# Causal attention and an FFN on one core: scores with queries on partitions, and DMA transposes of the exponentials

## The chip, the core and the metric

The kernel runs on one core of a Trainium2 chip. A core has five engines that run side by side, each with its own in-order queue of instructions: TensorE (PE) for matrix products, with the loading of its weights (PEld) shown apart; VectorE (DVE); ScalarE (ACT); GpSimd (POOL); and SyncE (SP), which here issues all DMAs. Engines wait for each other by semaphores. TensorE writes to PSUM, eight banks of 128 partitions by 512 float32 columns; the rest lives in SBUF, also in 128 partitions. A matrix product takes a weight tile of up to 128 x 128, and streams the columns of a second operand past it.

The metric is the device time of one execution in microseconds (us).

## What is computed

Eight sequences (B) of 576 tokens (S), eight heads (H) of 64 (D): causal softmax attention, mixed by a gate with a read from a memory; then a feed-forward network on all 4608 tokens. Inputs and weights are float32 or float64, and products are made of float16 parts that together hold more digits.

```python
def _attn_ref(q, k, v, M_prev, z_prev, beta):
    scores = scale * np.matmul(q, k.transpose(0, 1, 3, 2))
    scores = np.where(causal, -1000000000.0, scores)
    scores = scores - scores.max(-1, keepdims=True)
    a = np.exp(scores)
    a /= a.sum(-1, keepdims=True) + 1e-09
    local = np.matmul(a, v)
    q_p = phi(q)         # phi(x) = max(x, 0) + min(exp(x), 1)
    mem_out = einsum(q_p, M_prev) / (einsum(q_p, z_prev) + 1e-06)
    return g * mem_out + (1 - g) * local

def _moe_ref(x, w_in, w_out):          # x: 4608 x 512, w_in: 512 x 2048, w_out: 2048 x 512
    h = x @ w_in
    g = h * np.clip(h + 3.0, 0.0, 6.0) / 6.0
    return g @ w_out
```

## The kernel before

**Attention.** Queries go in blocks of 128 (the fifth of a sequence has 64). Heads come in pairs. A unit is some query blocks of one head: blocks 0 and 1 together, or one of blocks 2, 3, 4, so that a unit's scores fill one PSUM bank. A sequence has 4 x 8 = 32 units, in the order unit kind, pair, head. For sequences 1 to 7 the operands are float16: k and q as high and low parts, stacked so that one product with 128 rows holds both of k's parts. Sequence 0 runs in float32 while the weights are prepared.

A unit goes through these steps, each a method of `Unit`:

- `scores` (PE, L347, L348, L350): keys on the output's partitions, queries on its columns. For each block i and each key block j up to i, two products of 128 (or 64) columns; on the diagonal a third adds the mask (identity by `negm`). One of three banks (`ps_s`) holds the result, sT.
- `reduce` (DVE L360, ACT L358, POOL L362): the maximum over the key blocks, per partition and query; then a maximum over the partitions, which POOL also spreads to all of them (mb).
- `sub` (DVE L368): a = sT + shift - mb. `exp` (ACT L377) in place, and the high part ah in float16 (POOL L381).
- `lo` (DVE L389): the low part, al = a - ah.
- `pv` (PE L413 to L417): ah and al stand with keys on partitions, and so are weights for the products with v as they are. Per block and key block three products of 64 or 65 columns; then two with the memory. The 65th column of v is ones: the sum of the row.
- `combine` (DVE L430 to L432, L438; ACT L436, L437): division, gate, sum into x, for both heads of a pair.

**Preparation.** While a sequence runs, `prep_steps` brings the next one's pairs: loads of q, k, v (SP), absolute maxima (ACT, POOL), scales (DVE), splits into parts (ACT and DVE, L156, L157), and copies by DMA into one of six slots (four for k as `stack`, L210 and L211, four for q, L218, four for phi(q)). `PREP_AT` says in which unit each step is emitted.

**FFN.** 18 blocks of 256 tokens. A block has 16 pieces: 8 of `ffn1` (L523 to L525, 24 products of 256 columns each; then ACT L531, DVE L532, ACT L533, DVE L534), 8 of `ffn2` (L546 to L548, 12 products of 512 columns). Block 0 is float32. Its x comes as two float16 parts, moved to the transposed place by `dma_start_transpose` (SP, L496). W1 and W2 arrive as float64 words, are decoded on ACT and DVE (L622 to L626) and split (L157).

**Order.** The main loop emits, for unit t, its scores and reduction, for unit t-1 sub, exp and lo, for unit t-2 pv and combine, and in between FFN pieces at an even rate, attention `LEAD` = 40 pieces ahead. `at(...)` gives each piece of work a priority, and the Tile framework's scheduler makes of that the order of instructions on each engine. The last 80 pieces of the FFN are left to the end.

Of the kernel before, what the change touches and what calls it, by code (L numbers as in the profile page):

```python
# [12 lines left out]
F32 = mybir.dt.float32  # L13
# [40 lines left out]
PREP_AT = (  # L54
# [4 lines left out]
)  # L59
PREP_AT_0 = (  # L60
    (10, 11, 12, 12, 13, 14, 14, 15, 15, 15),
    (16, 17, 18, 18, 19, 19, 20, 20, 21, 21),
) + PREP_AT[2:]
LN_SA = float(np.log(SA))


@with_exitstack
def kernel(ctx, tc, qT, kT, v, mz, beta, w_in, w_out, out):
# [249 lines left out]
    class Unit:  # L318
# [56 lines left out]
        def exp(self):  # L375
            a = self.a[:, 0:self.n]
            ACT.activation(a, a, AF.Exp, scale=slots[self.b, self.p]["esc"])  # L377
            if self.b == 0:
                return
# [429 lines left out]
```

## Time and profile before

| | |
|---|---|
| runs | 1120.56 and 1121.33 us, median 1120.94 us |
| profiled execution | 1120.2 us from its first to its last instruction |
| ScalarE busy | 791.1 us (71%) |
| GpSimd busy | 412.2 us (37%) |
| HBM, DMA | 48.14 MB read, 9.44 MB written; 101.39 MB moved, mean 91 GB/s |

The profile is of one execution. The runs' times hold some tenths of a microsecond around the span. A group's row has: line, engine, operation, what it writes and reads, shapes, count, then busy time and the mean of one in ns, then the idle time of the engine just ahead of such instructions and what ended it. The row of slices shows the course: 40 slices of 28 us, each digit the busy share in tenths.

```profile
PE   8999999999999899999999999999999999999998
PEld 6888767586767667676768576867685868685664
DVE  5999889899899969998999988888799968893321
ACT  5787879677877778787877787668686857563321
POOL 3322223444444433554244533354344433341000
DMA  8734452333424343315332434233404230101100
```

DVE's load is near full until the last quarter, in which the attention has ended and the FFN alone runs on. Matmuls overlap each other, so that a full row of PE is not PE at its peak.

### The profile page before, as it was taken

What the parts mean: (1) busy time and instruction counts of PE and PEld (TensorE: products, weight loads), DVE (VectorE), ACT (ScalarE), POOL (GpSimd) and SP (SyncE); (2) the same over time, 40 slices, a digit from 0 to 9 for tenths busy, and PEclk for the clock granted to TensorE, in tenths of its full rate; (3) what the DMA queues carried; (4) which work ended last, traced back from release to release, by engine and by line L of the source; (5) the groups of instructions that cost most, each with busy time, mean ns of one, the idle gap of its engine ahead of it and who ended that gap; (6) DMA issues with size and microseconds to landing.
All of it is one profiled execution on the core that took longest, in us unless ns stands there. A gap on an engine that the chain in (4) does not pass through costs nothing.

```text
span 1120.2 us, 28768 instructions
## 1 busy us (share of the span) xinstructions
PE 1083.2 (97%) x10736; PEld 797.4 (71%) x10736; DVE 930.7 (83%) x2436; ACT 791.1 (71%) x1880; POOL 412.2 (37%) x544
## 2 busy tenths in 40 slices
PE   8999999999999899999999999999999999999998
PEld 6888767586767667676768576867685868685664
DVE  5999889899899969998999988888799968893321
ACT  5787879677877778787877787668686857563321
POOL 3322223444444433554244533354344433341000
PEclk9999999999999999999999999999999999999999
DMA  8734452333424343315332434233404230101100
GB/s 263 291 100 160 119 135 70 94 91 87 116 84 106 70 118 89 97 45 138 97 76 71 101 96 102 76 92 97 116 22 107 77 69 14 36 5 36 27 13 19
DMA packets 101468, 101.39 MB, mean 91 GB/s; under 512 B 50256, under 2 KB 80976, under 8 KB 101328
## 3 DMA queue, kind: packets, MB, share of 16 engines
q1 hardware_dynamic: 101328, 99.56, 33.1%
q8 instruction: 84, 1.38, 0.5%
q14 instruction: 56, 0.46, 0.1%
HBM read 48.14 MB, written 9.44 MB: 51 GB/s over the span
## 4 chain that ended last, share of the span: by engine, by line
PE 42%; DVE 32%; ACT 8%; issue 8%; DMA 6%; POOL 2%; SPq 1%; DVEq 0%; ACTq 0%; POOLq 0%
DVE a L368 6%; PE po L546 5%; PE po L548 5%; PE po L547 5%; PE ph L523 5%; DVE rm L360 5%; PE ph L524 4%; PE ph L525 4%; DVE al L389 4%; DVE r L532 3%; PE ph L518 3%; DVE g L534 2%; PE sT L343 2%; DVE W L157 2%; POOL mb L362 2%
## 5 line engine op out<-in xcount | busy, mean ns | idle before, releaser
L362 POOL PARTITION_ALL_REDUCE mb<-rm x256 | 251.7, 983 | 336.7 <-DVE rm L360 237.4
L523 PE MATMUL ph<-x,W 128*128 128x256 f16 x1088 | 297.6, 274 | 12.7 <-DVE r L532 7.3
L525 PE MATMUL ph<-x,W 128*128 128x256 f16 x1088 | 297.5, 273 | 0.0
L524 PE MATMUL ph<-x,W 128*128 128x256 f16 x1088 | 297.4, 273 | 0.0
L381 POOL TENSOR_SCALAR_AFFINE_SELECT ah<-a 128x384 f16<-128x384 f32 (+2 forms) x224 | 145.4, 650 | 214.4 <-ACT a L377 105.4
L546 PE MATMUL po<-W,g 128*128 128x512 f16 x544 | 206.6, 380 | 1.9 <-ACT ot L554 1.6
L548 PE MATMUL po<-W,g 128*128 128x512 f16 x544 | 206.5, 380 | 0.8 <-DVE g L534 0.8
L547 PE MATMUL po<-W,g 128*128 128x512 f16 x544 | 206.7, 380 | 0.0
L377 ACT ACTIVATE a<-a,scal 128x384 f32<-128x384 f32 (+2 forms) x224 | 141.6, 633 | 57.0 <-DVE a L368 48.8
L368 DVE SCALAR_TENSOR_TENSOR a<-sT,scal,mb 128x128 f32<-128x128 f32 (+4 forms) x280 | 147.2, 541 | 13.3 <-POOL mb L362 12.4
L360 DVE TENSOR_REDUCE rm<-sT 128x128 f32<-128x256 f32 (+3 forms) x256 | 135.6, 530 | 11.5 <-PE sT L350 4.6
L389 DVE TENSOR_TENSOR al<-a,ah 128x384 f16<-128x384 f32 (+2 forms) x224 | 134.0, 598 | 9.2 <-POOL ah L381 8.0
L532 DVE SCALAR_TENSOR_TENSOR r<-r,ph 128x512 f32<-128x512 f32 x136 | 92.1, 677 | 53.2 <-ACT r L531 52.6
L436 ACT ACTIVATE x<-o,cf 128x64 f32<-128x64 f32 (+1 forms) x320 | 100.6, 314 | 44.2 <-DVE cf L432 39.5
L531 ACT ACTIVATE r<-ph,bias_g,gsc 128x512 f32<-128x512 f32 x136 | 106.5, 783 | 34.2 <-PE ph L525 29.1
L347 PE MATMUL sT<-slot 128*128 128x128 f16 (+1 forms) x840 | 123.7, 210 | 3.9 <-DVE a L368 2.1
L348 PE MATMUL sT<-slot 128*128 128x128 f16 (+1 forms) x840 | 124.3, 210 | 0.0
L523 PEld LDWEIGHTS <-W 128*128 128x128 f16 x1088 | 106.8, 98 | 23.1 <-issue 6.6
L413 PE MATMUL o<-slot,ah 128*128 128x65 f16 (+1 forms) x840 | 116.3, 195 | 6.9 <-ACT y L437 3.6
L533 ACT ACTIVATE g<-r 128x512 f16<-128x512 f32 x136 | 86.4, 636 | 51.2 <-DVE r L532 51.1
L524 PEld LDWEIGHTS <-W 128*128 128x128 f16 x1088 | 106.7, 98 | 19.5 <-issue 5.0
L414 PE MATMUL o<-slot,ah 128*128 128x64 f16 (+1 forms) x840 | 115.4, 195 | 0.0
(149 smaller groups left out, 2387.4 us busy)
## 6 DMA issues: line engine op xcount, KB each, us to landing
slot<-q SPq DMA_DIRECT2D x112, 144.0 KB, 2.5
out<-ot SPq DMA_DIRECT2D x36, 256.0 KB, 2.0
stv<-vn SPq DMA_DIRECT2D x28, 320.0 KB, 3.3
W<-w_in SPq DMA_DIRECT2D x8, 1024.0 KB, 9.5
slot<-w_out SPq DMA_DIRECT2D x8, 1024.0 KB, 4.9
stq<-qT SPq DMA_DIRECT2D x28, 288.0 KB, 3.1
stk<-kT SPq DMA_DIRECT2D x28, 288.0 KB, 3.3
slot<-k SPq DMA_DIRECT2D x112, 72.0 KB, 2.0
```

The costliest lines, as they stand in the source:

```text
L360: DVE.tensor_reduce(rm[:, m0:m0 + nq], src.rearrange("p (t q) -> p q t", q=nq), axis=AX.X, op=ALU.max)
L362: POOL.partition_all_reduce(mb[:, 0:self.m], rm[:, 0:self.m], P, RMAX)
L368: DVE.scalar_tensor_tensor(a[:, c0:c0 + w].rearrange("p (t q) -> p t q", q=nq), self.sT[:, c0:c0 + w].rearrange("p (t q) -> p t q", q=nq), ...
L377: ACT.activation(a, a, AF.Exp, scale=slots[self.b, self.p]["esc"])
L381: POOL.affine_select(self.ah[:, 0:self.n], a, pattern=[[0, self.n]], compare_op=ALU.is_ge, fill=0.0, base=1, channel_multiplier=0)
L389: DVE.tensor_tensor(self.al[:, 0:n], self.a[:, 0:n], self.ah[:, 0:n], op=ALU.subtract)
L523: PE.matmul(ph[:, m], wh, f["xh"][:, c], start=c == 0, stop=False)
L524: PE.matmul(ph[:, m], wh, f["xl"][:, c], start=False, stop=False)
L525: PE.matmul(ph[:, m], wl, f["xh"][:, c], start=False, stop=c == 3)
L546: PE.matmul(po, gh[:, m, ts], W2[:, m, 0:512], start=m == 0, stop=False)
L547: PE.matmul(po, gh[:, m, ts], W2[:, m, 512:], start=False, stop=False)
L548: PE.matmul(po, gl[:, m, ts], W2[:, m, 0:512], start=False, stop=m == 15)
```

## The change

For sequences 1 to 7:

- **Scores with queries on partitions.** q is now the weight (`qst`, 128 rows with both parts of q), k streams past it (`khl`). Per query block two products of up to 512 columns. The mask products are gone. The fifth blocks of a pair's two heads make one unit (`both`): 64 queries of one head on partitions 0 to 63, of the other on 64 to 127, with two banks, for 512 and 64 columns. The unit of head 0 falls away (`idle`), so a sequence has 28 units.
- **One pass for mask, scale and maximum.** `tensor_tensor_reduce` on DVE adds a mask, multiplies by a negative scale and gives each row's minimum. In the order it stands as two ISA rows: the pass, and a read of its accumulator. A small DVE addition puts the logarithm of a constant in. The exponential takes the row's number as its bias: one ACT instruction per block. `sub` and the reduction over partitions on POOL remain for sequence 0 alone.
- **DMA transposes.** The exponentials now have queries on partitions, and `pv` needs keys there. So high and low part stand side by side in one tile (`a16`, three buffers), and one `dma_start_transpose` a unit writes them, block by block of 128 x 128, to one of four buffers (`aT_ring`): 6, 6, 8 or 10 blocks, 196 transposes in all. POOL clears 64 padding columns in the unit of the last blocks.
- **Order.** `pv` and `combine` come four units behind the scores (`PV_D`), not two. The last two unit kinds (blocks 3 and 4) are taken pair by pair: both kinds of one pair, then the next pair. Due times go by the columns of a unit. There are five slots instead of six, and `PREP_AT` gives other units. The second staging place of the second weights is the memory of the aT buffers.

On DVE, around the last eviction of FFN block 4 (r_4_14, its piece 7). Names hold sequence, unit kind, pair and head: rm_2_3_2_0 belongs to sequence 2, kind 3. Before:

```order
L389 TENSOR_TENSOR al_2_3_0_1_5650<-a_2_3_0_1_5611,ah_2_3_0_1_5614 128x320
L157 SCALAR_TENSOR_TENSOR qp_3_2_5852<-e_3_2_5848,s_3_2_5600,qp_3_2_5852 128x576
L431 RECIPROCAL cf_2_2_3_1_3_5557<-cf_2_2_3_1_3_5557 128x4
L532 SCALAR_TENSOR_TENSOR r_4_14_6007<-r_4_14_6007,ph_4_14_5982 128x512
L534 TENSOR_TENSOR g2_97<-r_4_12_5934,g2_97 128x512
L360 TENSOR_REDUCE rm_2_3_2_0_5812<-sT_2_3_2_0_5782 128x64
L368 SCALAR_TENSOR_TENSOR a_2_3_1_1_5777<-sT_2_3_1_1_5694,scal_2_1_2772,mb_2_3_1_1_5724 128x320
```

And now (nm is the row's number, s the scores):

```order
L388 ISA a_3_0_2_0_5727,nm_3_0_2_0_5728<-s_3_0_2_0_5707,mask_102,scal_3_2_5110 128x128
L388 ISA nm_3_0_2_0_5728 128x1
L388 ISA a_3_0_2_0_5727,nm_3_0_2_0_5728<-s_3_0_2_0_5707,mask_102,scal_3_2_5110 128x256
L388 ISA nm_3_0_2_0_5728 128x1
L510 TENSOR_TENSOR x_3_0_5780<-x_3_0_5780,y_3_0_0_1_0_5785 128x128
L504 TENSOR_TENSOR cf_3_0_0_1_1_5792<-cf_3_0_0_1_1_5792,coef_3_3642 128x4
L399 TENSOR_SCALAR nm_3_0_2_0_5728<-nm_3_0_2_0_5728 128x2
L604 SCALAR_TENSOR_TENSOR r_4_14_5470<-r_4_14_5470,ph_4_14_5445 128x512
```

The same eviction of the FFN stood in the last unit kind of sequence 2, and stands in the first of sequence 3; ahead of it DVE has 58 units' low parts before (32 and 26 of sequences 1 and 2) and 60 now (28, 28 and 4).

On SP, while pairs of the next sequence are brought. Before:

```order
L173 DMA stq_5_0_8527<-qT 128x576
L173 DMA stk_5_0_8529<-kT 128x576
L210 DMA slot1_103<-qp_4_3_8508 64x576 x2
L211 DMA slot1_103<-qp_4_3_8508 64x576 x2
L555 DMA out<-ot_6_1_9264 128x512
L175 DMA stv_5_0_8531<-vn 128x640
L210 DMA slot2_104<-k_5_0_8888 64x576 x2
```

And now:

```order
L183 DMA stq_4_1_6470<-qT 128x576
L183 DMA stk_4_1_6472<-kT 128x576
L455 DMA_TRANSPOSE aT_all_109<-a16_3_1_0_1_6072 128x6x128
L185 DMA stv_4_1_6474<-vn 128x640
L455 DMA_TRANSPOSE aT_all_109<-a16_3_1_1_0_6133 128x6x128
L627 DMA out<-ot_4_1_5979 128x512
L455 DMA_TRANSPOSE aT_all_109<-a16_3_1_1_1_6234 128x6x128
L455 DMA_TRANSPOSE aT_all_109<-a16_3_1_2_0_6290 128x6x128
```

The transposes stand between loads of the next sequence and stores of the FFN, and wait behind them where those wait.

```diff
+AB, A16B, ATB = 2, 3, 4
+PV_D = 4
-NSLOT = 6
+NSLOT = 5
...
+    mask = const.tile([P, 512], BF16, name="mask")
+    mask2 = const.tile([P, D], BF16, name="mask2")
-        sizes = [2 * NB * P, 4 * S, 2 * S, NB * 2 * 129]
+        sizes = [4 * S, 2 * S, 2 * S, NB * 2 * 129]
...
+    aT_all = const.tile([P, ATB * 2 * NB * P], F16, name="aT_all")
+    aT_ring = [aT_all[:, k * 2 * NB * P:(k + 1) * 2 * NB * P].rearrange("p (j q) -> p j q", q=P) for k in range(ATB)]
+    raw.append(aT_all[:, 0:4096])
...
+    class Unit:
+            self.both = b > 0 and u == LAST
+            self.idle = self.both and h == 0
+            self.heads = (0, 1) if self.both else (h,)
...
         def scores(self):
+            sl = slots[self.b, self.p]["sl"]
+            self.sT = [ps_s.tile([P, 512], F32, name=f"s_{self.id}", tag="sT")]
+            if self.both:
+                self.sT.append(ps_s.tile([P, 512], F32, name=f"s2_{self.id}", tag="sT"))
+            for i, nq, c0, _ in self.blocks:
+                for h in self.heads:
+                    r0 = D * h if self.both else 0
+                    w = min((i + 1) * P, S)
+                    for part in range(len(self.sT)):
+                        k0, k1 = 512 * part, min(512 * part + 512, w)
+                        o = self.sT[part][r0:r0 + nq, (c0 if part == 0 else 0):][:, 0:k1 - k0]
+                        for x in range(2):
+                            PE.matmul(o, qst[sl][:, h, i * P:i * P + nq], khl[sl][:, x, h, k0:k1],
+                                      start=x == 0, stop=x == 1)
...
         def reduce(self):
+            def masked(o, src, m, init, acc):
+                DVE.tensor_tensor_reduce(o, src, m, sd["nesc"], init, ALU.add, ALU.min, acc)
+            if self.both:
+                masked(a[:, 0:512], self.sT[0], mask[:, 0:1].broadcast_to([P, 512]), 3e38, nm[:, 0:1])
+                masked(a[:, 512:S], self.sT[1][:, 0:D], mask2, nm[:, 0:1], nm[:, 1:2])
+                DVE.tensor_scalar_add(nm[:, 2:3], nm[:, 1:2], LN_SA)
+                return
+            for k, (i, nq, c0, _) in enumerate(self.blocks):
+                w = (i + 1) * P
+                masked(a[:, c0:c0 + w], self.sT[0][:, c0:c0 + w], mask[:, 384 - i * P:512], 3e38, nm[:, k:k + 1])
+            k = len(self.blocks)
+            DVE.tensor_scalar_add(nm[:, 2:2 + k], nm[:, 0:k], LN_SA)
...
         def exp(self):
+            for k, (i, nq, c0, _) in enumerate(self.blocks):
+                a = self.a[:, c0:c0 + min((i + 1) * P, S)]
+                c = 2 + k
+                ACT.activation(a, a, AF.Exp, bias=self.nm[:, c:c + 1], scale=-1.0)
+            self.a16 = p2.tile([P, 2 * NB * P], F16, name=f"a16_{self.id}", tag="a16", bufs=A16B)[:, 0:2 * n]
+            self.hl = self.a16.rearrange("p (x n) -> p x n", x=2)
+            if self.both:
+                POOL.memset(self.hl[:, :, S:], 0.0)
+            POOL.affine_select(self.hl[:, 0, 0:self.m], self.a[:, 0:self.m], pattern=[[0, self.m]],
+                               compare_op=ALU.is_ge, fill=0.0, base=1, channel_multiplier=0)
...
         def lo(self):
+            DVE.tensor_tensor(self.hl[:, 1, 0:m], self.a[:, 0:m], self.hl[:, 0, 0:m], op=ALU.subtract)
+            nb = 2 * self.n // P
+            self.aT = aT_ring[aT_n[0] % ATB]
+            aT_n[0] += 1
+            SP.dma_start_transpose(out=self.aT[:, 0:nb], in_=self.a16)
...
         def pv(self):
+                        ah = self.aT[:, c0 // P + j, r0:r0 + nq]
+                        al = self.aT[:, (self.n + c0) // P + j, r0:r0 + nq]
...
+        order = [(u, p, h) for u in range(2) for p in range(NP) for h in range(2)]
+        order += [(u, p, h) for p in range(NP) for u in (2, 3) for h in range(2)]
```

More of the change, by code (lines that the diff above doesn't have):

```diff
@@ L200, in scale @@
             eps = scal[:, 2:4].unsqueeze(1).broadcast_to([P, 2, 2])
-            esc, shift = scal[:, 0:1], scal[:, 1:2]
-            slots[b, p] = dict(sl=sl, esc=esc, shift=shift, coef=coef, eps=eps)
+            slots[b, p] = dict(sl=sl, nesc=scal[:, 0:1], coef=coef, eps=eps)
         def pair_tiles(nm):
@@ L314 @@
     UNITS = [(0, 1), (2,), (3,), (4,)]
+    LAST = len(UNITS) - 1
     xtiles = {}
@@ L328, in __init__, with scores_t @@
             self.id = f"{b}_{u}_{p}_{h}"
[L330 removed]
+        def scores_t(self):
             h = self.h
[L332 to L335 removed]
+            t = nat[self.p]
             sT = self.sT = ps_s.tile([P, 512], F32, name=f"sT_{self.id}", tag="sT")
@@ L349, in scores @@
+                    PE.matmul(o, t["k"][r, j * P:(j + 1) * P], t["q"][r, q0:q0 + nq],
+                              start=True, stop=j < i)
                     if j == i:
                         PE.matmul(o, ident16, negm[:, 0:nq], start=False, stop=True)
-        def reduce(self):
-            rm = p1.tile([P, 256], F32, name=f"rm_{self.id}", tag="rm")
-            mb = self.mb = p2.tile([P, 256], F32, name=f"mb_{self.id}", tag="mb")
+        def scores(self):
+            if self.idle:
+                return
+            if self.b == 0:
+                self.scores_t()
+                return
+            sl = slots[self.b, self.p]["sl"]
[12 more added lines that the diff above has]
+                                      start=x == 0, stop=x == 1)
@@ new lines, in reduce @@
+        def reduce(self):
+            if self.idle:
+                return
+            if self.b == 0:
+                self.reduce_t()
+                return
+            a = self.a = p2.tile([P, S], F32, name=f"a_{self.id}", tag="a", bufs=AB)
+            nm = self.nm = small.tile([P, 4], F32, name=f"nm_{self.id}", tag="nm", bufs=6)
+            sd = slots[self.b, self.p]
+            def masked(o, src, m, init, acc):
[4 more added lines that the diff above has]
+                DVE.tensor_scalar_add(nm[:, 2:3], nm[:, 1:2], LN_SA)
+                return
+            for k, (i, nq, c0, _) in enumerate(self.blocks):
[3 more added lines that the diff above has]
+            DVE.tensor_scalar_add(nm[:, 2:2 + k], nm[:, 0:k], LN_SA)
@@ L661 @@
     DVE.tensor_copy(negm, negf)
+    POOL.memset(mask[:, 0:384], 0.0)
+    POOL.memset(negf, 0.0)
+    POOL.affine_select(negf, negf, pattern=[[-1, P]], compare_op=ALU.is_ge, fill=-3e38, base=0,
+                       channel_multiplier=1)
+    DVE.tensor_copy(mask[:, 384:], negf)
+    for r in range(2):
+        DVE.tensor_copy(mask2[D * r:D * r + D], negf[D * r:D * r + D, D * r:D * r + D])
     DVE.memset(bias_g, TG / 2.0)
@@ L695, in w2_scale @@
         wsc["i12"] = i12
-    units = [Unit(b, u, p, h) for b in range(B) for u in range(len(UNITS))
-             for p in range(NP) for h in range(2)]
+    units, due_at = [], []
+    first = []
+    for b in range(B):
+        order = [(u, p, h) for u in range(2) for p in range(NP) for h in range(2)]
+        order += [(u, p, h) for p in range(NP) for u in (2, 3) for h in range(2)]
+        first.append(len(units))
+        new = [x for x in (Unit(b, *o) for o in order) if not x.idle]
+        work = [x.n * len(x.heads) * (0.5 if x.both else 1.0) for x in new]
+        at_ = 0.0
+        for x, w in zip(new, work):
+            units.append(x)
+            due_at.append((b + at_ / sum(work)) * S * 16 / TB)
+            at_ += w
     NU = len(units)
-    upb = NU // B
+    first.append(NU)
     plan = {}
@@ L706, in due @@
     def due(t):
-        b, k = divmod(t, upb)
-        u, k = divmod(k, 2 * NP)
-        tok = [sum(rows[i] for i in g) for g in UNITS]
-        return (b * S + sum(tok[:u]) + tok[u] * k / (2 * NP)) / TB * 16 - (LEAD if t >= 2 * NP else LEAD0)
+        return due_at[t] - (LEAD if t >= 2 * NP else LEAD0)
     def ffn_piece():
@@ L729, in ffn_piece @@
         return True
-    for t in range(NU + 2):
+    for t in range(NU + PV_D):
         if t < NU:
             u = units[t]
-            if t % upb == 0 and u.b + 1 < B:
+            if t in first and u.b + 1 < B:
                 ms, ps = mem_steps(u.b + 1), [prep_steps(u.b + 1, p) for p in range(NP)]
@@ L738 @@
                 for p, ks in enumerate(PREP_AT if t else PREP_AT_0):
+                    last = max(x for x in range(t, first[u.b + 1]) if units[x].p == p - 1) if p else 0
+                    assert not p or ks[5] + t > last + PV_D
                     for f, k in zip(ps[p], ks):
@@ L754 @@
             units[t].scores()
-        if t >= 2:
-            at(due(t - 2))
-            units[t - 2].pv()
+        if t >= PV_D and t - PV_D < NU:
+            at(due(t - PV_D))
+            units[t - PV_D].pv()
         if t < NU:
@@ L767 @@
             units[t - 1].lo()
-        if t >= 2:
-            at(due(t - 2))
-            units[t - 2].combine()
+        if t >= PV_D and t - PV_D < NU:
+            at(due(t - PV_D))
+            units[t - PV_D].combine()
         if t >= X_T:
```

105 lines of the change are left out of this document (50 added, 55 removed), and 11 rows, old and new, of tables (PREP_AT, PREP_AT_0).

## Prediction

> **What bounds the kernel now.** I read the page first, then the windows and the chain of waits stage by stage, then the shapes of DVE's groups.
>
> ```profile
> span 1120.2 us, 28768 instructions
> PE 1083.2 (97%) x10736; PEld 797.4 (71%) x10736; DVE 930.7 (83%) x2436; ACT 791.1 (71%) x1880; POOL 412.2 (37%) x544
> 160.00:860.00 700.00, 675.84 (x7467) 495.86 (x7466) 639.19 (x1716) 538.88 (x1311) 302.88 (x402) 1.00 0.35 91
> 387.00:860.00 473.00, 460.77 (x5070) 336.22 (x5067) 424.30 (x1151) 360.16 (x883) 202.89 (x271) 0.99 0.36 92
> 860.00:1015.00 155.00, 153.72 (x1808) 115.25 (x1806) 129.87 (x334) 101.02 (x245) 62.43 (x90) 1.00 0.19 42
> by line: issue 10.5%; DVE a L368 8.0%; DVE rm L360 6.9%; DVE al L389 6.4%; DVE r L532 4.4%; DVE g L534 4.0%; PE po L546 3.5%; PE po L548 3.4%; PE po L547 3.4%; POOL mb L362 2.8%; PE ph L523 2.7%; PE ph L524 2.6%; PE ph L525 2.6%; DVE W L157
> by line: PE ph L523 13.4%; PE ph L525 13.3%; PE ph L524 13.3%; PE po L548 10.7%; PE po L547 10.6%; PE po L546 10.4%; PE sT L347 4.7%; PE sT L348 4.6%; PE o L413 4.1%; PE o L415 3.7%; PE o L414 3.2%; PE o L417 1.9%; PE sT L350 1.6%; DVE al L
> ```
>
> The window rows give PE, PEld, DVE, ACT, POOL busy in that order. The two chain rows are those of 387 to 860 and of 860 to 1015. In the first, DVE is busy 424 of 473 us (90%) and its lines lead the chain: DVE holds the pace. In the second, DVE is at 84% and the chain is 95.5% PE. So PE stands close behind DVE, and what DVE saves is cut off by PE. "PE 97%" says little, because matmuls overlap. I take PE's need from starts, first and last of a run:
>
> ```profile
> 499.92 0.27 PE L523 MATMUL ph<-x,W 128*128 128x256 f16 x1
> 500.80 0.27 PE L525 MATMUL ph<-x,W 128*128 128x256 f16 x1
> ...
> 501.12 0.38 PE L548 MATMUL po<-W,g 128*128 128x512 f16 x1
> 503.28 0.38 PE L546 MATMUL po<-W,g 128*128 128x512 f16 x1
> ...
> 504.02 0.19 PE L348 MATMUL sT<-slot 128*128 128x64 f16 x1
> 504.23 0.19 PE L347 MATMUL sT<-slot 128*128 128x64 f16 x1
> ...
> 530.08 0.22 PE L347 MATMUL sT<-slot 128*128 128x128 f16 x1
> 530.48 0.22 PE L350 MATMUL sT<-negm,ident 128*128 128x128 bf16 x1
> ```
>
> Eight, ten, seven and seven steps: 0.110 us for 256 columns, 0.216 for 512, 0.030 for 64, 0.057 for 128. A short matmul costs nearly only its columns. One FFN block (192 of 256, 96 of 512) needs 41.9 us of PE, a sequence of attention 26.9 (per head 20 score products of 128 columns and 10 of 64, five masks, 55 of 65 columns at 0.031).
>
> **Scores, masks (PE).** Per head 35 products become 12: two each of 128, 256, 384 (0.16) and 512 columns, and for the last block two of 512 and two of 64. That is 1.58 us against 1.66: 0.7 us a sequence, 5 in all. Fewer instructions, the same columns.
>
> **The reduction (DVE, POOL).**
>
> ```profile
> L360 DVE TENSOR_REDUCE rm<-sT 128x128 f32<-128x256 f32 (+3 forms) x256 | 135.6, 530 | 11.5 <-PE sT L350 4.6 <-ACT rm L358 4.0 <-POOL mb L362 2.2
> L368 DVE SCALAR_TENSOR_TENSOR a<-sT,scal,mb 128x128 f32<-128x128 f32 (+4 forms) x280 | 147.2, 541 | 13.3 <-POOL mb L362 12.4
> L389 DVE TENSOR_TENSOR al<-a,ah 128x384 f16<-128x384 f32 (+2 forms) x224 | 134.0, 598 | 9.2 <-POOL ah L381 8.0
> L368 DVE SCALAR_TENSOR_TENSOR a<-sT,scal,mb 128x512 f32<-128x512 f32 x56 | 41.5, 740 | 2.4 <-POOL mb L362 2.2
> L368 DVE SCALAR_TENSOR_TENSOR a<-sT,scal,mb 128x128 f32<-128x128 f32 x56 | 19.2, 342 | 4.3 <-POOL mb L362 4.3
> L431 DVE RECIPROCAL cf<-cf 128x4 f32<-128x4 f32 (+1 forms) x160 | 25.5, 166 | 0.7
> L197 DVE TENSOR_SCALAR scal<-s,s_m 128x1 f32<-128x1 f32 x28 | 5.6, 200 | 0.0
> L152 ACT ACTIVATION_READ_ACCUMULATOR junk<-x 128x1 f32 (+1 forms) x40 | 8.2, 205 | 0.0
> L362 POOL PARTITION_ALL_REDUCE mb<-rm x256 | 251.7, 983 | 336.7 <-DVE rm L360 237.4
> 499.79 0.68 DVE L532 SCALAR_TENSOR_TENSOR r<-r,ph 128x512 f32<-128x512 f32 x1
> 500.39 0.26 DVE L432 TENSOR_TENSOR cf<-cf,coef 128x4 f32<-128x4 f32 x1
> ```
>
> The last two rows show that a DVE instruction starts 0.08 us before the one ahead ends, so each costs its duration less 0.08. Before, a head has 4 reductions, 5 subtractions, 4 low parts: 2.12 + 2.71 + 2.39 - 13 x 0.08 = 6.18 us. After, one pass makes the masked sum and the row's minimum. It is not in the trace. I price it like L368, which reads the same scores and one operand more: 342 ns plus 1.036 per column over 128, so 2.16 us for blocks 0 to 3, and half of 1.02 for the last (a pair shares it): 2.67 - 5 x 0.08 = 2.27. Behind each stands a read of the accumulator (in the order an ISA row with one column out): between nothing and ScalarE's 205 ns; I take DVE's small L431, so 5 x 0.086 = 0.43. The sum with the logarithm is L197's kind: 3.5 x 0.12 = 0.42. Low parts: 3.5 instructions, 32 columns fewer: 2.01. Together 5.13: 1.05 us saved a head, 8.4 a sequence, 59 in all. Ends for the pass: no gain below L360's 530 mean; above, two passes instead of one, 1.62 us a head more. POOL loses 224 of L362 (220 us) and is not near a bound; what leaves is 1 us out of each unit's way.
>
> **Exponentials (ACT).**
>
> ```profile
> L377 ACT ACTIVATE a<-a,scal 128x384 f32<-128x384 f32 x112 | 69.7, 624 | 23.1 <-DVE a L368 21.9 <-DVE coef L199 0.9 <-DVE cf L430 0.2
> L377 ACT ACTIVATE a<-a,scal 128x512 f32<-128x512 f32 x56 | 40.5, 724 | 15.3 <-DVE a L368 12.4 <-DVE cf L432 1.9 <-DVE cf L431 0.7
> L358 ACT ACTIVATE rm<-sT 128x128 f32<-128x128 f32 x64 | 17.8, 278 | 6.1 <-POOL mb L362 3.7 <-PE sT L350 2.2
> ```
>
> The first unit's one exponential of 384 columns becomes two (about 0.42 + 0.52 for 0.62: +18 us), the last blocks' are joined (-10), the copy L358 goes for sequences 1 to 7 (-16): -8 us, and ACT is at 77% in 160 to 860. Nothing.
>
> **Transposes, SP's queue.**
>
> ```profile
> L496 SPq DMA_TRANSPOSE x<-W x46: 1194/1264/2816, 147.1 to 1060.4; - x46
> DMA to landing us min/median/max: 2.7/3.2/4.8
> q1 hardware_dynamic: 101328, 99.56, 33.1%
> SPq L555 <- ACT ot L554: 191.4, 25, 28.1
> SPq L210 <- ACT k L156: 150.4, 20, 20.9
> ```
>
> There are 196 new ones with 6 to 10 blocks of 128 x 128, 1400 blocks in all. The trace has 8 blocks: 1.26 us of SP to issue, 3.2 to land. So a sequence adds 35 us to SP's queue, which has some 45 us of issues in 120: it fits. The DMA engines move 45.9 MB more (1400 blocks of 32 KB); at q1's own rate that is 15% of the span, at 3.2 us for eight blocks with all engines held it is at most 560 us, 50%: with 35% in 160 to 860 still under one. A unit's way grows by 3.2 and loses POOL's 0.98 and L368's 0.54, about +2 us; pv now comes four units later instead of two, and a unit takes 120/28 = 4.3 us, so this is covered unless SP holds a transpose back. q and k only swap their four copies each; five slots move do_k behind the pair that leaves; the pad of 64 columns is 28 POOL memsets, the new masks a few short operations while the first loads land. All of that I cost at nothing, under the same cover. Pair by pair, the fourth and fifth blocks of a sequence's x are complete only with its last pair, so FFN block 1 comes later; that is in the next sum, since it is counted up to block 4.
>
> The Trainium skill ("VectorE: DVE Perf Modes", The three transpose paths) gives 1309 ns for one 128 x 128 block by DMA. By that, eight blocks would take 10.5 us where the row has 3.2, and the sum would be the rival at the end of the next part. The trace disagrees with it for blocks of one instruction.
>
> **Where the order puts it, and the sum.** DVE's last eviction of FFN block 4 is the 32nd L532:
>
> ```profile
> L532 DVE SCALAR_TENSOR_TENSOR r<-r,ph x32: 650/675/689, 178.3 to 386.4; 128x512 f32<-128x512 f32 x32
> ```
>
> It ends at 387.0. Ahead of it DVE has 58 of 32 units a sequence (1.81 sequences) before, and 60 of 28 (2.14) after: attention runs further ahead. DVE up to there: 1.81 x 49.4 = 89.5 before, 2.14 x 41.0 = 88.0 after, plus five more splits (3.7) and six combines (3.2): +5.3, at 91% occupancy +6. So this point comes at 393, not earlier: the saving is spent on running ahead. Behind it PE needs 13.5 blocks (565 us) and 5.19 sequences (140) before: 705 of 733 us, 28 idle. After: 565 + 4.86 x 26.2 = 692. DVE then has about 81% in the attention part, under the 84% of 860 to 1015, where what isn't PE is 4.5% at most. I take 2% of some 600 us: 12 idle. **393 + 692 + 12 = 1097 us**, against a span of 1120.2 and runs of 1120.94 in the median (0.7 apart, left out).
>
> **Rivals.**
> - Full relief: running ahead costs DVE nothing before block 4, and PE idles nowhere behind it: 387 - 1.81 x 8.4/0.91 = 370, and 705 - 5.19 x 0.7 = 701 of PE: 1071. For it: DVE leads the chain from 160 to 860. Against: the order above. 0.15.
> - Transposes come late. SP is in order, and single waits of 28 and 21 us stand in it; four buffers give a unit 4 x 4.3 = 17 us. Each microsecond beyond costs 196/4 = 49 us: half a microsecond eats the gain (1120), one makes 1145. Against: the order sets them by when their inputs come. 0.17 (0.12 within 2%, 0.05 slower).
> - Slower: the masked pass takes two cycles a column. 1.62 - 1.05 = +0.57 us a head, 32 us of DVE, which at 91% holds the pace longer: about 1155. It decides from 1.05/1568 = 0.67 ns a column above L368's 1.04 on. No row of this kind; L368 and L360 both read once. 0.07.
> - The saving is all spent on running ahead, and waits between engines stay: 1112 to 1118. 0.05.
> - The transposes go one block at a time, each as long as L496's whole issue, 1.26 us: 1400 x 1.26 = 1764 us. Against: the landing row, 3.2 us for eight. 0.01. This is the rule of the Trainium skill cited above; with its figure it would be 1833 us.
>
> **How the numbers follow.** Forecast 0.55, from 1080 (no idle, cheap reads) to 1115 (reads of 205 ns, idle as before); 1098.5 cuts it: 0.30 faster, 0.25 within 2%. Two per cent is about what a measurement of this kernel can tell from no change. Faster 0.30 + 0.15 = 0.45; same 0.25 + 0.12 + 0.05 = 0.42; slower 0.05 + 0.07 + 0.01 = 0.13. The range, 1070 to 1132, leaves out the two-pass case, the late end of the transposes and the low end of the full relief.
>
> **What would show it.** DVE's busy sum near 870; the masked pass 0.34 at 128 and 0.74 at 512 columns; the accumulator read under 0.2; block 4's last eviction at 385 to 400; PE leading the chain from there; waits of pv for aT under 15 us in sum. A block 4 much before 385, a pass above 1 us at 512 columns, or PE waiting for aT by tens of microseconds would make it wrong.

## The result, and the profile after

The changed kernel takes 1164.41 us in the median of two runs (1160.9 and 1167.91), the kernel before 1120.94 beside it: a ratio of 1.040, with a 95% interval from 1.031 to 1.048. It is slower, where 1097 us was forecast and 1132 was the top of the range. (A run's time lies 1.7 us over the span of its profile, as 1167.91 over 1166.2.) One execution of the run sync_held below, 1160.23 us, was of a slower state; its median and its ratio leave it out, but its profile is of that execution.

First the page of the changed kernel, then its groups by shape. L388 is the masked pass with the read of its accumulator, L399 the small addition.

```profile
span 1166.2 us, 26514 instructions
PE 1088.1 (93%) x9448; PEld 756.9 (65%) x9448; DVE 831.6 (71%) x2628; ACT 784.5 (67%) x1852; POOL 191.5 (16%) x323
q1 hardware_dynamic: 286800, 145.46, 57.9%
PE 23%; DMA 3%; DVE 2%; ACT 1%; SPq 1%; issue 1%; POOL 0%; DVEq 0%; ACTq 0%
```

```profile
L388 DVE CUSTOM_DVE_ANT_0 a<-s,mask,scal 128x512 f32<-128x512 f32 x84 | 62.6, 746 | 7.6 <-PE s L374 6.5
L388 DVE CUSTOM_DVE_ANT_0 a<-s,mask,scal 128x128 f32<-128x128 f32 x56 | 19.4, 346 | 2.3 <-PE s L374 1.5
L388 DVE DVE_READ_ACCUMULATOR2_ANT nm<- 128x1 f32 x280 | 23.2, 83 | 0.0
```

The relief is there, and for DVE larger than forecast: its busy time fell from 930.7 to 831.6 us, GpSimd's from 412.2 to 191.5. Yet the span grew by 46 us. No engine but TensorE is busier than before, and that by 5 us; the DMA engines' share rose, from 33.1% to 57.9%. (The chain of this page could be followed for a third of the span only, so it settles nothing.) Where the time went shows in the windows: those of the prediction, and one of 40 us that was not looked at then. Columns are PE, PEld, DVE, ACT, POOL busy, TensorE's granted clock, DMA share, GB/s. After:

```profile
387.00:860.00 473.00, 442.87 (x4241) 302.35 (x4238) 355.73 (x1206) 341.78 (x831) 79.31 (x143) 0.99 0.66 135
860.00:1015.00 155.00, 150.41 (x1491) 104.38 (x1488) 115.06 (x365) 102.88 (x238) 23.23 (x46) 1.00 0.54 107
160.00:200.00 40.00, 23.40 (x184) 14.62 (x182) 32.01 (x125) 32.74 (x85) 7.18 (x14) 0.66 0.67 139
```

And before:

```profile
160.00:200.00 40.00, 36.56 (x353) 27.42 (x352) 36.95 (x101) 34.67 (x82) 12.93 (x15) 1.00 0.32 86
```

There are two losses. From 160 to 200 us TensorE is busy 23 us where it was busy 37. And in the steady part, 387 to 860, neither DVE (75%) nor ScalarE (72%) is near full, and still TensorE has 30 us idle where it had 12. The evictions of the FFN (L604, before L532) date both. These rows count the evictions of block 1 and of blocks 1 to 4 in the changed kernel; the last number is the start of the last one.

```profile
L604 DVE SCALAR_TENSOR_TENSOR r<-r,ph x8: 669/680/690, 199.5 to 236.2; 128x512 f32<-128x512 f32 x8
...
L604 DVE SCALAR_TENSOR_TENSOR r<-r,ph x32: 668/682/690, 199.5 to 425.9; 128x512 f32<-128x512 f32 x32
```

Block 1 ends at 236.9 us (before 208.0), block 4 at 426.5 (before 387.0, forecast 393), and behind it come 739.7 us (before 733.1, forecast 704).

TensorE waits for transposed parts: in the view of the tile aT_all, from 200 us on,

```profile
  DMA aT_all<-a: 75.8, 73
...
  PEld L485: 43.3, 44
  PE o L485: 32.5, 29
  POOL a L444: 17.6, 5
```

All of it stands before the products of L485, with which a unit's pv begins. The first row adds the waits of two queues, and they are mostly the same ones: the loading of the weights waits (43 us), and the product behind it with it (33 us). By their times the two together cover 43 us. So TensorE waits 33 to 43 us for aT, not 76; the prediction's limit was 15. The prediction had a rival of that kind, and priced it 1120 to 1145.

### The profile page after: what moved, and what is told of

It is laid out like the page before. It is cut to its first block, busy times and chain, and to the rows that moved or that the text cites. A ratio compares the mean times of both kernels' runs of the same rounds, so it can differ in the third digit from the quotient of the medians.

```text
span 1166.2 us, 26514 instructions
## 1 busy us (share of the span) xinstructions
PE 1088.1 (93%) x9448; PEld 756.9 (65%) x9448; DVE 831.6 (71%) x2628; ACT 784.5 (67%) x1852; POOL 191.5 (16%) x323
## 3 DMA queue, kind: packets, MB, share of 16 engines
q1 hardware_dynamic: 286800, 145.46, 57.9%
## 5 line engine op out<-in xcount | busy, mean ns | idle before, releaser
L444 POOL TENSOR_SCALAR_AFFINE_SELECT a<-a 128x384 f16<-128x384 f32 (+2 forms) x196 | 124.7, 637 | 588.1 <-ACT a L437 545.3
L437 ACT ACTIVATE a<-a,nm 128x128 f32<-128x128 f32 (+4 forms) x252 | 139.8, 584 | 47.8 <-DVE nm L399 31.6
L451 DVE TENSOR_TENSOR a<-a,a 128x384 f16<-128x384 f32 (+2 forms) x196 | 125.8, 643 | 56.5 <-POOL a L444 56.2
L388 DVE CUSTOM_DVE_ANT_0 a<-s,mask,scal 128x128 f32<-128x128 f32 (+2 forms) x252 | 139.1, 568 | 14.3 <-PE s L374 12.0
L485 PE MATMUL o<-slot,aT_all 128*128 128x65 f16 (+1 forms) x840 | 104.5, 196 | 40.4 <-DMA aT_all<-a 36.5
L604 DVE SCALAR_TENSOR_TENSOR r<-r,ph 128x512 f32<-128x512 f32 x136 | 92.8, 682 | 58.7 <-ACT r L603 57.7
L595 PEld LDWEIGHTS <-W 128*128 128x128 f16 x1088 | 108.4, 100 | 34.0 <-DMA x<-W 6.6
L374 PE MATMUL s<-slot 128*64 128x64 f16 (+5 forms) x672 | 115.0, 303 | 16.3 <-DVE nm L388 15.0
L596 PEld LDWEIGHTS <-W 128*128 128x128 f16 x1088 | 108.4, 100 | 24.8 <-issue 5.1
L485 PEld LDWEIGHTS <-aT_all 128*128 128x128 f16 (+1 forms) x840 | 80.2, 101 | 61.3 <-DMA aT_all<-a 49.7
L597 PEld LDWEIGHTS <-W 128*128 128x128 f16 x1088 | 108.4, 100 | 15.2
L606 DVE TENSOR_TENSOR g<-r,g 128x512 f16<-128x512 f32 x136 | 94.0, 692 | 21.9 <-ACT g L605 21.4
L486 PE MATMUL o<-slot,aT_all 128*128 128x64 f16 (+1 forms) x840 | 103.7, 196 | 0.0
```

Source lines behind the costliest of these rows:

```text
L374: PE.matmul(o, qst[sl][:, h, i * P:i * P + nq], khl[sl][:, x, h, k0:k1], start=x == 0, stop=x == 1)
L388: DVE.tensor_tensor_reduce(o, src, m, sd["nesc"], init, ALU.add, ALU.min, acc)
L437: ACT.activation(a, a, AF.Exp, bias=self.nm[:, c:c + 1], scale=-1.0)
L444: POOL.affine_select(self.hl[:, 0, 0:self.m], self.a[:, 0:self.m], pattern=[[0, self.m]], compare_op=ALU.is_ge, fill=0.0, base=1, channel_ ...
L451: DVE.tensor_tensor(self.hl[:, 1, 0:m], self.a[:, 0:m], self.hl[:, 0, 0:m], op=ALU.subtract)
L485: PE.matmul(o, ah, vv[:, j, h, 0:D + 1], start=j == 0, stop=False)
```

## Experiments

Theory A: in the new order the fourth block of sequence 0 is complete only with the last pair, so FFN block 1 gets its x late and TensorE starves. Theory B: a transpose's way ahead of pv is longer than the order allows for. A third, queue theory, came up on the way. All runs are set against the kernel before, measured among them (1119.0 to 1122.0 us). Each edit gives the scheduler another order of instructions, so a few microseconds between two runs need not be the edit's own. The changed kernel's own ratio is known to some 9 us only, so a difference of 10 us to it is not clear of noise. "SyncE" is the sum of the durations of SyncE's DMA instructions over the trace, worked out from all of them.

| run | median us | ratio to before (95%) | SyncE us |
|---|---|---|---|
| before | 1120.94 | | 362 |
| changed | 1164.41 | 1.040 (1.031 to 1.048) | 630 |
| before_pairs | 1134.32 | 1.013 (1.010 to 1.015) | |
| kinds_seq0 | 1146.08 | 1.022 (1.020 to 1.024) | 632 |
| no_transposes | 1121.51 | 1.002 (0.999 to 1.005) | 348 |
| no_transposes_kinds_seq0 | 1099.21 | 0.982 (0.979 to 0.985) | 349 |
| plain_copies | 1133.43 | 1.012 (1.010 to 1.014) | 460 |
| later_pv | 1153.00 | 1.029 (1.026 to 1.033) | 629 |
| later_pv_five_buffers | 1153.80 | 1.029 (1.025 to 1.033) | |
| later_pv_kinds_seq0 | 1135.88 | 1.013 (1.009 to 1.018) | |
| later_pv_kinds_five_a | 1130.67 | 1.009 (1.007 to 1.010) | |
| later_pv_kinds_five_b | 1138.57 | 1.014 (1.010 to 1.019) | |
| idle_transposes | 1153.53 | 1.030 (1.026 to 1.033) | 626 |
| idle_small_packets | 1136.16 | 1.013 (1.011 to 1.015) | 492 |
| sync_held | 1152.07 | 1.025 (1.020 to 1.030) | 724 |
| copies_on_gpsimd | 1173.08 | 1.045 (1.043 to 1.048) | 432 |
| joined_transposes | 1142.77 | 1.021 (1.017 to 1.024) | 572 |
| joined_kinds_seq0 | 1139.76 | 1.017 (1.012 to 1.022) | 564 |
| copies_left_out | 1121.08 | 1.000 (0.999 to 1.002) | 451 |
| no_transposes_no_copies | 1108.51 | 0.989 (0.986 to 0.992) | 173 |

**The order alone, put into the kernel before.**

```diff
+        order = [(u, p, h) for u in range(2) for p in range(NP) for h in range(2)]
+        order += [(u, p, h) for p in range(NP) for u in (2, 3) for h in range(2)]
```

> The kernel before, with only the order of units taken from the changed one: the last two unit kinds of each sequence pair by pair, due times by columns. Keys stay on partitions, and there are no transposes of exponentials. Theory A (pair by pair, the fourth block of sequence 0 is complete only with its last pair, FFN block 1 waits for it, and TensorE starves from 160 to 200 us): the last eviction of FFN block 1 moves from 207.7 to 225-237 us, and the run ends 15 to 29 us later, at 1135 to 1150. Theory B (the stall at 160 to 200 comes from the transposes and their landings): block 1 stays within 5 us of 207.7, and the time within 5 us of 1120.9.

It costs 13 us, with no transpose of exponentials in the kernel; block 1 moves to 221.8 us:

```profile
L532 DVE SCALAR_TENSOR_TENSOR r<-r,ph x8: 651/676/689, 192.0 to 221.1; 128x512 f32<-128x512 f32 x8
```

The time is a little under theory A's range, but the order's cost is seen without transposes. Not all of it need be the late block 1: in this order DVE has 61 units' low parts ahead of block 4's last eviction instead of 58, and is busy 357 us up to there instead of 350.

**The order of sequence 0 undone in the changed kernel.**

```diff
+        order += ([(u, p, h) for p in range(NP) for u in (2, 3) for h in range(2)] if b else
+                  [(u, p, h) for u in (2, 3) for p in range(NP) for h in range(2)])
```

> The changed kernel, with sequence 0 alone taken kind by kind again; the preparation of sequence 1's pairs 1 to 3 comes later by some units, since their slots are left later. Theory A: the last eviction of FFN block 1 comes at 205 to 218 us instead of 236.6, and the run ends at 1135 to 1147 (20 to 29 us earlier than 1164.4). Theory B: block 1 stays beyond 230, time 1160 to 1168. A third outcome: block 1 is early, but the later slots of sequence 1 give the gain back, with the end beyond 1155.

The edit also moves the preparation of sequence 1's pairs 1 to 3 to later units (`PREP_AT_0`), since their slots come free later. 18 us come back. TensorE is busy again from 160 to 200, but in the next 160 us it is idle for 19.4, where the changed kernel had 14.5:

```profile
160.00:200.00 40.00, 35.17 (x361) 26.68 (x361) 37.38 (x135) 37.97 (x95) 7.11 (x12) 1.00 0.59 130
200.00:360.00 160.00, 140.56 (x1399) 93.61 (x1398) 132.43 (x457) 122.72 (x305) 36.44 (x59) 0.96 0.79 156
```

So theory A holds for the stall itself. The 5 us may be the third outcome, the later slots; without transposes, below, the same edit costs nothing there (9.9 us idle, then 9.3), so the later slots alone don't do it.

**The transposes taken away, or made plain copies.**

```diff
-            self.a16 = p2.tile([P, 2 * NB * P], F16, name=f"a16_{self.id}", tag="a16", bufs=A16B)[:, 0:2 * n]
+            self.a16 = aT_all[:, k * 2 * NB * P:k * 2 * NB * P + 2 * n]
...
-            SP.dma_start_transpose(out=self.aT[:, 0:nb], in_=self.a16)
```

> The changed kernel without the 196 transposes: high and low parts are written straight into the four buffers, and pv takes them as they are (its weights are then not the transposed exponentials; all products are there). Theory A alone: the stall at 160 to 200 stays, FFN block 1 ends beyond 228, and the time is above 1155. Theory B (each unit's way through the transposes holds TensorE up, 86 us of waits for aT): 1120 to 1145, with TensorE's gaps per 40 us falling from about 4.4 to 2.5 after 240 us.

```diff
-            SP.dma_start_transpose(out=self.aT[:, 0:nb], in_=self.a16)
+            SP.dma_start(aT_all[:, k * 2 * NB * P:k * 2 * NB * P + nb * P], self.a16)
```

> The changed kernel with each transpose replaced by a plain DMA of the same bytes to the same buffer (pv's weights are then not the transposed exponentials). If any stop at SyncE's queue and a landing of some us cost as much (in-order queue, four units between), the time stays within 8 us of the changed kernel, 1156 to 1172. If the transposition itself is what costs (its 3.2 us landing, its 1.25 us of issue, its packets beside the loads), the time is within 8 us of the run without transposes.

All that hangs on the transposes costs 43 us. Part of it is at the start: without them block 1 ends at 214.3 us instead of 236.9, in the same order. (Such a date is that of one trace: no_transposes_no_copies below, the same program up to there, has 227.5.) A plain DMA in the same place, on the same queue, costs 12, between what the two theories had said, so not any stop on the way costs 43. The order of sequence 0 and the transposes, both taken away by the two edits above:

> No transposes (pv takes the parts untransposed) and sequence 0 kind by kind, both in one kernel. If the two costs are separate, 43 and 18 us, the time is 1164.4 - 61 = 1100 to 1107, which would also be near the 1097 of the prediction, whose sum counted neither. If the transposes were part of the stall at 160 to 200 (block 1 already came at 214.0 without them, against 236.6), the two overlap: 1110 to 1118.

1099.2 us. Alone, the two edits gave 43 and 18 us, together they give 65, so the two costs add up. Without them the time is the forecast's; how much of that is luck, the next section asks.

**Is it pv's wait?** The order of TensorE tells what theory B rests on: at the spacings of the prediction, the median of TensorE's own work between a unit's last score product and its first pv product is some 12 us, not 17. Due times of pv six pieces later make it some 20:

```diff
-            at(due(t - PV_D))
+            at(due(t - PV_D) + (6 if units[t - PV_D].b else 0))
             units[t - PV_D].pv()
```

> The changed kernel with one number added: pv of sequences 1 to 7 is due six FFN pieces later than before, nothing else. By the order, the median of TensorE's own work between a unit's scores and its pv grows from some 12 us (least 6 to 9 for kinds 1 to 3) to 19-23 us (least 11), where the way through DVE, ScalarE, GpSimd, SyncE and the transpose's landing takes 12 to 14 us. Theory B (the cover was too short: in the order pv stands 12 us behind, not the 17 us of four units): the waits of pv for aT fall from 86 to under 25 us, and the time to 1128-1145; the stall at 160 to 200 us stays. Rival (four buffers, three tiles for the parts and three score banks are the limit, not pv's place): the waits turn up at SyncE's transposes and at the scores instead, time 1155 to 1170.

The waits fall as expected (from 43 to 13 us, counted as above, after 200 us), the time only by 11, to 1153.0, where 1128 to 1145 was expected. Other waits take their place, GpSimd's for a tile of parts among them (17.6 us in the changed kernel):

```profile
POOL a L444 <- DMA aT_all<-a: 78.2, 23, 8.4
```

A fifth buffer was meant to free them:

```diff
-AB, A16B, ATB = 2, 3, 4
+AB, A16B, ATB = 2, 3, 5
```

> The run later_pv (pv due six pieces later) with five buffers for transposed parts instead of four. In later_pv the waits of pv for aT fell from 86 to 32 us, but GpSimd's waits for a tile of parts behind a transpose rose from 18 to 78 us, and SyncE waited some 60 us for pv to leave a buffer. If those four buffers gave the gain back: GpSimd's waits fall below 40 us and the time to 1135-1147. If they are beside the path: 1148 to 1157, as with four.

It gave nothing, and GpSimd's waits fell to 67 us only. So a fifth buffer for transposed parts isn't what was lacking; more than three tiles for the parts ahead of the transpose were not tried. Then pv's wait was taken away altogether, and all else of the transposes kept:

```diff
+            t = p2.tile([P, 2 * NB * P], F16, name=f"t16_{self.id}", tag="a16", bufs=A16B)
+            SP.dma_start_transpose(out=t.rearrange("p (j q) -> p j q", q=P)[:, 0:nb], in_=self.a16)
```

> The run without transposes, with all 196 transposes issued again behind the low parts, but into three tiles that nobody reads (pv takes the parts untransposed). SyncE's queue, the DMA engines' load and the packets are as in the changed kernel; only pv doesn't wait for a landing. If the way is what costs (issue and landing ahead of pv): within 8 us of the run without transposes, 1114 to 1130. If contention costs (SyncE's queue held 1.25 us a piece, DMA engines at 0.66 beside the loads): 1145 to 1165.

1153.5 us: transposes whose result nobody uses cost 32 of the 43 us. Theory B fell to some 11 us, about what later_pv gave back, and 11 is hardly clear of noise. Something that the transposes hold up costs the rest.

**SyncE's queue or the DMA engines?** Two runs take the two apart: one DMA a unit in the transposes' packet size, and three DMAs of 128 bytes.

```diff
+            SP.dma_start(t[:, 0:1260].rearrange("p (j q) -> p j q", q=140)[:, 0:nb, 0:P],
+                         self.a16[:, 0:nb * P].rearrange("p (j q) -> p j q", q=P))
```

> The run without transposes, with one plain DMA a unit behind the low parts, into tiles that nobody reads: the same bytes in pieces of 256 bytes, as the transposes' packets have (9 of the 10 blocks in the last kind; pv takes the parts untransposed). An issue of about 0.5 us on SyncE instead of 1.25. If packets at the DMA engines cost: near the run with idle transposes, 1142 to 1158. If SyncE's held queue costs: under 1134, since 0.5 us a unit is what the plain copies held.

```diff
+            for c in range(3):
+                SP.dma_start(t[0:1, D * c:D * c + D], self.a16[0:1, D * c:D * c + D])
```

> The run without transposes, with three DMAs of 128 bytes a unit behind the low parts, into tiles that nobody reads: some 1.3 to 1.6 us of SyncE's issue per unit and next to no traffic (pv takes the parts untransposed). If SyncE's held queue costs: 1142 to 1158, as the idle transposes. If packets cost: 1116 to 1130.

These rows give how long an instruction holds SyncE, in ns (least, median, most), first in the changed kernel:

```profile
L455 SPq DMA_TRANSPOSE aT_all<-a x196: 1209/1247/2553, 173.4 to 1056.7; - x196
L218 SPq DMA_DIRECT2D slot<-q x56: 461/548/1364, 125.6 to 920.6; - x56
L231 SPq DMA_DIRECT2D slot<-k x112: 590/617/1335, 129.1 to 922.6; - x112
```

in idle_small_packets:

```profile
L457 SPq DMA_DIRECT2D t<-aT_all x196: 593/607/1437, 175.3 to 1027.6; - x196
```

and in sync_held:

```profile
L457 SPq DMA_DIRECT2D t<-aT_all x588: 497/587/1922, 173.2 to 1051.5; - x196
```

"Held" is the time that an instruction takes on SyncE. Next to no traffic, but SyncE held 588 x 0.59 = 345 us, costs 26 us by the ratios and 31 by the medians over the run without transposes (its executions spread from 1142.8 to 1153.6), where the idle transposes cost 32. The bytes of the transposes in packets of their size, with a hold of 0.61 us a unit, cost 15; 1136.2 lies between the two ranges, nearer to that of the queue. So a held queue is enough for a loss of this size, without any traffic. That the traffic has no share at all isn't shown: sync_held holds SyncE longer (724 us against 626) and costs no more. At its price, the 278 us more of the idle transposes would cost 19 to 23, so some 10 of their 32 may be something else.

Two rivals are smaller. SyncE's waits in front of these instructions, summed over the views, are 295 us in idle_small_packets, 352 in idle_transposes and 103 in sync_held (whose DMAs read high parts alone, and so needn't wait for the low ones): they don't go with the cost. And GpSimd waits until the idle DMA has read a unit's parts, 35, 37 and 27 us in these three runs: that is the same where the cost is 15 and where it is 32.

**Freeing the queue.** Three runs keep the transposes. The first moves the copies into the slots to another engine:

```diff
-                SP.dma_start(dst[0:D, h, :S], hi[D * h:D * h + D])
-                SP.dma_start(dst[D:P, h, :S], lo[D * h:D * h + D])
+                POOL.dma_start(dst[0:D, h, :S], hi[D * h:D * h + D])
+                POOL.dma_start(dst[D:P, h, :S], lo[D * h:D * h + D])
```

> The changed kernel with its transposes, and the 336 copies of the parts of k, q and phi(q) into the slots issued by GpSimd instead of SyncE: some 195 us of issue (336 times 0.58) leave SyncE's queue, the traffic stays. If SyncE's held queue costs: 1135 to 1150. If packets cost: 1157 to 1170; above that, GpSimd's own issues hold up the high parts behind them.

SyncE is freed of 198 us, and the kernel is no faster (ratios of 1.045 and 1.040, the latter uncertain by 0.008). GpSimd's queue is in order too, and the high parts stand in it behind copies that wait:

```profile
POOL slot L231 <- DMA slot<-k: 45.4, 31, 4.1
POOL slot L218 <- ACT q L166: 39.9, 21, 4.0
POOL slot L218 <- ACT qp L166: 23.6, 16, 5.5
```

So this run says nothing against the queue; it moved the blocking to an engine on the units' way. The Trainium skill ("Perfetto Trace Analysis", DMA Optimizations) says that balancing DMAs over the engines that can issue them may help where generating their descriptors is the bottleneck; here it didn't.

The second joins the transposes of a pair's two heads (and has the later pv):

```diff
+            if self.last:
+                SP.dma_start_transpose(out=self.aT[:, 0:nb], in_=self.pair16[:, 0:nb * P])
```

> A correct kernel: the run later_pv with one transpose for a pair's two heads (12, 12 and 16 blocks at once; the last kind as before), 112 transposes instead of 196. A transpose of 6 blocks holds SyncE 1.23 us and one of 10 blocks 1.37, so a joined one some 1.4 to 1.6, and SyncE is held some 90 us less. If SyncE's queue costs: 8 to 14 us under later_pv's 1153.0, 1138 to 1146. If not: 1150 to 1160, since the first head's parts now wait for the second's.

```profile
L463 SPq DMA_TRANSPOSE aT_all<-a x112: 1253/1478/3613, 176.1 to 1030.0; - x112
```

10 us less than later_pv, within the range of the queue theory, with 57 us less on SyncE, though the first head's parts now wait for the second's. The edit also makes the tiles and buffers hold a pair, two and three of them, so there is more room than before; the run doesn't tell the two apart. The third leaves copies out, from pair 1 of sequence 2 on (here of q and phi(q); those of k in the same way):

```diff
-            for h in range(2):
+            for h in range(2 if NP * b + p < NP + NSLOT else 0):
```

> The changed kernel with its transposes, but from the ninth prepared pair on (sequence 2, pair 1) the twelve copies of k, q and phi(q) into the slot are left out; the products take what the slot held before. 276 copies of 0.58 us are 160 us less on SyncE, all behind some 250 us. If SyncE's held queue costs, at 32 us for 278 us of issue: 18 us less, 1140 to 1152; the start stays (block 1 beyond 228). If pv's wait for a landing or the order on TensorE alone costs: 1158 to 1170.

1121.1 us, 43 less, more than twice of what was expected. Block 1 stays late (it ends at 230.2 us); in the profiled executions 7 us of the gain are there by then, 19 by the end of block 4 (407.1) and 49 at the end, so most of it comes later than the start. Pv's waits for aT, again of both queues, fall with the queue's load from 75.8 to 32.0 us, without any change in pv's place:

```profile
  DMA aT_all<-a: 32.0, 41
```

But copies also hold tiles that ScalarE waits for, so a control left the same copies out where there are no transposes:

> The run without transposes (pv takes the parts untransposed), and from the ninth prepared pair on without the copies of k, q and phi(q) into the slots. If the copies cost because the transposes crowd SyncE's queue: little is left to gain, 1110 to 1121. If they cost by themselves: 1075 to 1095, and copies_left_out says nothing on the queue.

13 us. The four runs make a square: with both 1164.4, without copies 1121.1, without transposes 1121.5, without both 1108.5. Each alone costs 13 us, both together 56: 30 us, give or take some 10 by the intervals, come only where both are there. They share SyncE's queue, and the DMA engines too; that it is mostly the queue is argued from sync_held and idle_small_packets.

How a late SyncE reaches TensorE was not tried step by step. In the traces ScalarE, in order too, waits longer for the next sequence's loads (stq, stk, stv, stm), with exponentials behind it: from 200 to 1060 us 28.5 us in no_transposes, 29.7 in idle_small_packets, 48.6 in idle_transposes and 63.6 in sync_held. Of these, in idle_transposes:

```profile
ACT junk L162 <- DMA stv<-vn: 24.1, 14, 4.5
```

in no_transposes:

```profile
ACT junk L162 <- DMA stv<-vn: 14.2, 9, 3.1
```

and in sync_held:

```profile
ACT junk L162 <- DMA stv<-vn: 30.9, 15, 4.3
ACT junk L162 <- DMA stq<-qT: 22.5, 13, 4.3
```

**Towards a faster kernel.** What helped was put together, by the edits above (five_a: pv four pieces later instead of six):

> Transposes kept, a correct kernel: pv due six pieces later and sequence 0 kind by kind. Theory A and B together: 1146 less 20 to 30 us, 1114 to 1128, about the kernel before or a little under. Rival (buffers are the limit): 1140 to 1150.

> A correct kernel: sequence 0 kind by kind, pv due four pieces later, five buffers. If start, cover and buffers add up: 1146 - 10 (later) - 10 (buffers) = 1118 to 1130. If four pieces are too few: 1130 to 1140.

> The same with pv due six pieces later. If buffers gave the gain back with four: 1112 to 1126 (with four it was 1135.9). If not: 1130 to 1138.

> The same with sequence 0 kind by kind, a correct kernel. If the costs add up: 1135.9 less 8 to 14 us, 1120 to 1129, level with the kernel before. If not: 1133 to 1142.

The best of those that leave nothing out is later_pv_kinds_five_a, 1130.7 us, still 0.9% over the kernel before. The gains don't add up in these, and all four runs lie over the ranges that this would have given (five_a by less than 1 us): with sequence 0 kind by kind, 200 to 360 us stays thin (TensorE 140 of 160 us busy in joined_kinds_seq0 too), and joining, which gave 10 us alone, gave none. No version that beats the kernel before was found.

## Why the prediction was wrong

**The reduction was right.** The pass takes 346 ns at 128 columns and 746 at 512, against 342 and 740. The read takes 83 ns and starts 76 ns before the pass ends (median), so it ends 8 ns behind it, where 86 ns each was taken: 280 x 0.078 = 22 us more relief. With the 59 of the sum that is 81 of the 99 us by which DVE fell; the other 18 are spread over small groups and were not followed. So its kind was right, and its size too small by two fifths. GpSimd fell by 221 us, 220 were forecast.

**The sum was met once the two losses were gone, its first term by luck.** Its two terms were block 4's last eviction at 393 us and 692 + 12 = 704 behind it. In no_transposes_kinds_seq0

```profile
L603 DVE SCALAR_TENSOR_TENSOR r<-r,ph x32: 654/676/690, 172.1 to 392.1; 128x512 f32<-128x512 f32 x32
```

that eviction ends at 392.7, and 1099.8 - 392.7 = 707.1 us follow. Behind block 4 it is as the prediction put it, TensorE holds the pace: the same window as above has it busy for all but 4.5 us:

```profile
387.00:860.00 473.00, 468.48 (x4514) 319.06 (x4511) 377.05 (x1266) 360.80 (x866) 82.22 (x152) 1.00 0.38 92
```

Up to block 4 it is not. The sum had DVE's work there grow by 5.3 us, since running ahead was to eat the saving. The windows up to that eviction, first in the kernel before, then in no_transposes_kinds_seq0, have DVE (the third of the busy times) at 349.7 and 341.5 us:

```profile
0.00:387.00 387.00, 369.29 (x3192) 282.20 (x3193) 349.67 (x907) 298.96 (x702) 146.54 (x182) 1.00 0.44 127
0.00:392.80 392.80, 374.39 (x3011) 272.71 (x3012) 341.47 (x1049) 317.34 (x766) 93.77 (x137) 1.00 0.49 135
```

So DVE's work fell by 8 us although attention runs ahead as foreseen (59 units' low parts, where 60 were counted): the relief was larger than taken. By the prediction's own rule the point should have come some 9 us earlier than 387, near 378. It came at 393 because DVE was busy 87% of the time up to there, where it was 90% before. Two errors of some 15 us cancel; what DVE waits for up to there was not followed. (A small slip besides: at the spacings shown, a head's 35 products before take 1.70 us, not 1.66, which moves the forecast by less than 1 us.)

What made the forecast wrong are the two things that the sum held at nothing.

**First failed step: "a sequence adds 35 us to SP's queue, which has some 45 us of issues in 120: it fits".** The sum was right (630 - 362 = 268 us more, 7 x 35 = 245 forecast), the conclusion wrong. SyncE works in order, and what stands behind a waiting or issuing instruction waits with it, however free the queue is later. That was priced at nothing, and came to 43 us together with the next point. The prediction asked only whether SP would hold a transpose back. The larger part is the reverse: transposes hold back what is not a transpose, 32 of 43 us without any reader (some 10 of them perhaps by other ways, as said above). So the rival "transposes come late" had the right place, but its condition was one of two, and its price, 1120 to 1145, lacked the 18 to 22 us of the order on top.

**Within it, the cover of four units.** pv stands four units later in the code, 4 x 4.3 = 17 us; in the order that the due times give, only some 12 us of TensorE's work lie between. The way takes as long: in the trace the median from a unit's last score product to the landing of its transpose is 11.9 us too. That cost some 11 us, as later_pv and idle_transposes agree, with the noise said above.

**Second failed step: "that is in the next sum, since it is counted up to block 4".** The sum counted DVE's work up to block 4, and the order of sequence 0 doesn't change that: DVE is busy 339.9 us up to there in the changed kernel and 340.8 in kinds_seq0. What grew was a wait: with x of block 1 late, TensorE has only sequence 1's units to run, and 40 us pass at 58% busy. In all, the order costs 13 us in the kernel before, 18 in the changed one, 22 without transposes. Only a part of that is lost at the start: by the end of block 4, kinds_seq0 is 12 us ahead of the changed kernel (414.1 and 426.5), and without transposes the same edit is 6 us ahead (392.7 and 399.2). The rest comes behind block 4, and its cause stays open. A sum of an engine's work holds a late input only where the engine is full.

**The other rivals.** A pass of two cycles a column, and transposes one block at a time, did not come: the pass is above, and a whole transpose's landing stayed at 3.2 us in the median.

## What to carry to other kernels

An in-order queue that issues for several streams has no free capacity just because its issues sum to less than the span: what counts is what stands behind each held or waiting instruction, and new traffic belongs on it only with a look at those behind. An order that finishes a tensor's parts later moves every consumer of the whole tensor, which a sum of work doesn't show: follow the first consumer by its inputs. When a change brings two parts, a run that takes both away tests the sum itself; but a total that is met proves little, until each of its terms is compared with the trace.

## What the runs showed of the hardware that was not expected

- A DMA's issue holds SyncE almost regardless of size: 0.59 us for 128 bytes on one partition, 0.61 for six to nine blocks of 128 x 128 in 256-byte pieces, 0.48 for six to ten blocks in long rows (plain_copies). A transpose holds it 1.23 us at 6 blocks, 1.28 at 8, 1.37 at 10 (medians by unit kind in the changed kernel), and 1.48 in the joined run, most of whose transposes have 12 or 16. So fewer and larger transposes are cheaper for the queue.
- Where TensorE starves, its granted clock falls too: 0.66 from 160 to 200 us with 23.4 us busy, 1.00 in the kernel before with 36.6 busy. The Trainium skill ("TensorE: Matmul & The Clock Gate", the part on the HAM clock gate) says that an idle array is gated to half its clock; the row agrees in direction. What of the loss at the start is due to the slower clock was not measured.
